# One channel of seven batches, loaded by itself and transformed in one run

## The chip, the cores and the metric

The kernel runs on one core of a Trainium2 chip. The core has five engines that work side by side and wait for each other by semaphores: TensorE (PE; its weight loads are listed apart as PEld), VectorE (DVE), ScalarE (ACT), GpSimd (POOL), and SyncE (SP), which here only issues DMAs. The DMAs run on 16 DMA engines. The metric is the time of one execution on the device in microseconds (us), the median of several runs.

## What is computed

The input x has 8 batches of 3008 rows and 256 columns ("channels"). Each batch goes through a Fourier transform over its rows and one over its channels, of which the real part is kept; the result goes, row by row, through a gated network:

```python
X = np.fft.fft(x, axis=1)
X = np.fft.fft(X, axis=2)
y = X.real.reshape(8 * 3008, 256)
gate = np.maximum(y @ w_gate, 0.0)      # 256 -> 1536
val  = y @ w_val
out  = gate * val @ w_out               # 1536 -> 256
```

## The kernel before

The transform over the channels is folded into the weights (tiles WA, WB, WM). The transform over the rows is done as matrix products with tables of cosines and sines (`tabC`, `tabS`). Before these products the rows of a batch are folded: rows 1, 2, 3, ... of the first half (tile XD, loaded in order) are added to the same rows counted from the end (tile XG, "mirrored", loaded from a reversed copy `xr` in DRAM), then halves are added and subtracted (tile AA, also called PQ), and channels d and 256 - d are added (tiles F) and subtracted (tiles G). So 128 or 129 channels are left of 256; 128 of them are the stationary operand of the products. Channel 128 is its own mirror image; it is the 129th and has no room in the 128.

For that channel batches 1 to 7 have products of their own. POOL computes `c128p` from column 128 of XG (line 187) and writes it, with signs, into the tile FN (line 188), in the slot of the batch. FN holds batches in pairs. For each pair, TensorE runs 12 products (line 656, `nyquist_steps`): 6 pieces of rows by 2 families of output rows, each with 4 stationary columns and 376 or 377 moving columns of `tabC`. Their results are copied to a small tile N (line 665, ScalarE; line 663, VectorE, once) and written to the DRAM tensor `ch` (lines 672 and 673, `keep_nyquist`), from where each batch reads its row (lines 1052 and 1055). The runs of 12 stand in batch 0 (for batch 1), and in batches 1, 3 and 5 (for the next two each). In batches 1, 3 and 5 they come after 18 of the 24 steps of the next batch's transform; the table `DFT_ODD` says after which tile of the network how many steps are done, `DFT_EVEN` the same for the other batches.

The order of instructions on each engine is written out by hand (a manual schedule): the generator lists steps of several kinds (`todo_dft`, `todo_out`, `todo_fold`), and after each tile of the network takes some from each list. Every engine then works through its own list in order. The folds of batches 1 and 2 are put on POOL at once during batch 0 (`run_fold(99)`), those of later batches step by step behind POOL's part in each tile (line 971), by an estimated cost written beside each step.

SP issues nearly all DMAs, in the order in which the generator came to them: loads of XD (lines 94 and 100), the reversed copies (`reverse`, line 133, two batches ahead), their one-row complement (`reverse_0`, line 137), loads of XG (line 142), output rows (line 754) and the rows of channel 128. Eight semaphores go round: each DMA waits until the one eight places before it has landed. Four buffers hold output rows on their way out (tile os, line 744).

During batch 0, `turns_and_rows` (line 490) issues the loads for batch 1 and the reversed copy for batch 2.

The functions that the change touches:

Of the kernel before, what the change touches and what calls it, by code (L numbers as in the profile page):

```python
# [34 lines left out]
def kernel(  # L35
# [46 lines left out]

    FF = [single(f"F{i}", [128, 2, 3, 2, 129], BF16) for i in range(2)]
    GG = [single(f"G{i}", [128, 2, 3, 2, 128], BF16) for i in range(2)]
    FN = single("FN", [128, 2, 3, 2, B // 2, 2, 2], BF16)

# [33 lines left out]
    def load_upward(t, r, queue):  # L122
        first = H - 128 - 128 * t - r * (H // 2)
        queue.dma_start(out=XG[:, r, t, :, :].rearrange("p a d -> p (a d)"), in_=pairs[first:first + 128, :])

    PC, NC = 64, 6
    xr = nc.dram_tensor("xr", (B, 2, NC, PC, 2 * D), F32).ap()
# [49 lines left out]
    def fold_steps(b):  # L177

        e, p, ts = nc.gpsimd, slice(0, 128), slice(0, 3)
        steps = [(1.1, lambda r=r, t=t: fold_a(e, p, r, t)) for t in range(3) for r in range(2)]  # L180
        if b == 1:
            steps.insert(0, (0.0, lambda: e.tensor_copy(go[:, 1:2], go[:, 0:1])))
        steps += [(0.2, lambda: e.tensor_tensor(XG[:, :, :, ::-1, 0], XG[:, :, :, ::-1, 0], XD[:, :, :, :, 0], op=ALU.add))]

        def channel_128():
            for i in range(2):
                e.tensor_tensor(c128p[:, i], XG[:, 0, :, ::-1, 128], XG[:, 1, :, ::-1, 128], op=SIGN[i])
            e.tensor_tensor(FN[:, :, :, :, b // 2, :, b % 2].rearrange("p i t q h -> p i (t q) h"),
                            c128p[:].rearrange("p i t q -> p i (t q)").unsqueeze(3).to_broadcast([128, 2, 6, 2]), sg[:], op=ALU.mult)
        steps.append((0.5, channel_128))  # L190
        if b + 1 < B:
            steps.append((0.0, lambda: reverse_0(b + 1) if b else None))
        for t in range(3):
            for i in range(2):
                steps.append((1.1, lambda i=i, t=t: fold_pq(e, p, i, t)))
                if (t, i) == (1, 0) and b + 1 < B:
                    steps.append((0.0, lambda: (load_rows(b + 1), load_last(b + 1))))

        def small():
            for i in range(2):  # L200
                e.tensor_tensor(PQ[:, i, :, :, 0], XG[:, 0, :, ::-1, 0], XG[:, 1, :, ::-1, 0], op=SIGN[i])
            zero = PQ[:, :, :, :, 0:1].rearrange("p i t q d -> p (i t q) d")
            e.tensor_tensor(FF[b % 2][:, :, :, :, 0:1].rearrange("p i t q d -> p (i t q) d"), zero, zero, op=ALU.add)
        steps.append((0.6, small))
        last = []
        for fam in (1, 0):
            last.append((1.7, lambda fam=fam: fold_f(e, p, ts, fam, b)))
            last.append((1.7, lambda fam=fam: fold_g(e, p, ts, fam, b)))
        if b + 1 < B:
            last.insert(3, (0.0, lambda: load_reversed(b + 1)))  # L210
        if b + 2 < B:
            last.append((0.0, lambda: reverse(b + 2)))
        return steps + last
# [22 lines left out]
    kvec = single("kvec", [128, NK])  # L236
    dvec = single("dvec", [128, 129], pool=st_)
    go = single("go", [128, 2])
    c128p = single("c128p", [128, 2, 3, 2])
    sg = single("sg", [128, 2, 6, 2])  # L240

    odd_k, even_k = slice(NE, NK), slice(0, NE)
    order, even_order = (1, 0, 3, 2, 5, 4), (1, 3, 5, 0, 2, 4)
# [84 lines left out]
    quotient(2)  # L328
    nc.vector.scalar_tensor_tensor(us[:, 5:6], in0=pidx[:], scalar=120.0, in1=us[:, 5:6], op0=ALU.is_lt, op1=ALU.mult)
    nc.vector.memset(FN[:], 0.0)  # L330
    quotient(5)
    quotient(4)
    nc.vector.memset(XD[96:128, :, 2, 1, :], 0.0)
# [98 lines left out]
    iota(kvec[:, 0:NE], [[2, NE]], 0, 0)  # L432
    nc.gpsimd.memset(sg[:], 2.0)
    for i in range(2):
        nc.gpsimd.memset(sg[:, i, 0::2, i:i + 1], -2.0)
    spare = AA[:].rearrange("p r t q d -> p (r t q d)")

    def even_turns(n, c):
# [51 lines left out]
    def turns_and_rows():  # L490
        load_rows(1)
        load_last(1)
        load_mirror_0(1)
        for n, c in enumerate(even_order):
            even_turns(n, c)
            if n == 1:
                minus_v(nc.gpsimd, 1)
            if n:
                load_mirror(1, (n - 1) // 2, (n - 1) % 2)
        load_mirror(1, 2, 1)  # L500
        reverse(2)

# [137 lines left out]
                    steps += part  # L642
        return steps

    def nyquist_steps(g, N):

        def one():
            if not paired:
                flush()
            d = psD.tile([128, 512], F32, name="d", tag="d")  # L650
            for k in range(6):
                t, par = k // 2, k % 2
                rows = slice(0, ROWS[par][t])
                for fam in range(2):
                    p, cols = slice(32 * fam, 32 * fam + 4), (slice(0, NE), slice(NE, NK))[fam]
                    nc.tensor.matmul(d[p, 0:NE - fam], lhsT=FN[rows, fam, t, par, g].rearrange("p s b -> p (s b)"),  # L656
                                     rhs=tabC[rows, 2 * t + par, cols], start=(k == 0), stop=(k == 5))

            def keep():
                for fam in range(2):  # L660
                    p = slice(32 * fam, 32 * fam + 4)
                    if fam and not paired:
                        nc.vector.tensor_scalar(N[p, 0:NJ], d[p, 0:NJ], scalar1=1.0, op0=ALU.mult, scalar2=None)
                    else:
                        nc.scalar.copy(N[p, 0:NE - fam], d[p, 0:NE - fam])
            evict.insert(0, keep)
        return [one]

    def keep_nyquist(g, N):
        W = 4 * NJ + 1  # L670
        for fam in range(2):
            nc.sync.dma_start(out=dram(ch128, 2 * g * W + 2 * (1 - fam) * NJ, [[NJ, 2], [W, 2], [1, NJ]]), in_=N[32 * fam:32 * fam + 4, 0:NJ])
        nc.sync.dma_start(out=ch128[2 * g:2 * g + 2, 4 * NJ:4 * NJ + 1], in_=N[2:4, NJ:NE])

    def new_uv():
        return [up.tile([128, 4 * NJ + 2], BF16, name=n, tag=n) for n in ("U", "V")]
# [104 lines left out]
    def gate_128():  # L781
# [2 lines left out]
            nc.tensor.matmul(p[:, f:f + 1], lhsT=WB[0][0:1, f * 128:(f + 1) * 128], rhs=one[:], start=True, stop=True)  # L784
        nc.vector.tensor_scalar(b2[:], p[:, 0:NF], scalar1=1.0, op0=ALU.mult, scalar2=None)
    more[(2, 2)] = [gate_128]

    DFT_0 = (0, 0, 0, 0, 0, 3, 0, 0, 4, 3, 3, 0), (0, 0, 0, 0, 0) + (1,) * 7, (3, 3, 3, 3, 3, 3, 0, 0, 0, 0, 0, 0)

    DFT_EVEN = (3, 0, 3, 0, 0, 0) * 4 + (0,) * 12  # L790
    DFT_ODD = (3, 0, 3, 0, 0, 0) * 3 + (1, 0, 3, 0, 3, 0, 0) + (0,) * 11
    todo_out, todo_dft, todo_fold = [], [], []
    credit, paired = 0, False
    pending = None
# [221 lines left out]
    for b in range(B):  # L1016
# [4 lines left out]
        for blk, block in enumerate(blocks):  # L1021
# [13 lines left out]
            if blk == (0 if b else 2) and b + 1 < B:  # L1035
                Un, Vn = new_uv()
                todo_dft = dft_steps(b + 1, Un, Vn, (1, 0), now=not b)
                CBn = up.tile([128, 4 * NJ + 2], BF16, name="CB", tag="CB")
                uv[b + 1] = Un, Vn, CBn
                steps, todo_dft = todo_dft, []  # L1040
                if b == 0 or b % 2:
                    g, N = (b + 1) // 2, rp.tile([36, NE], BF16, name="N", tag="N", bufs=1)
                    todo_dft = nyquist_steps(g, N)

                    def keep(N=N, g=g):
                        flush()
                        keep_nyquist(g, N)
                    first = 0 if b == 0 else 18
                    steps[first] = lambda step=steps[first], keep=keep: (keep(), step())

                def row_128(b=b, CBn=CBn):
                    nc.sync.dma_start(out=CBn[:, 0:4 * NJ + 1], in_=dram(ch128, (b + 1) * (4 * NJ + 1), [[0, 128], [1, 4 * NJ + 1]]))

                def row_0(b=b, Vn=Vn):
                    nc.sync.dma_start(out=Vn[0:1, 0:4 * NJ + 1], in_=ch128[b + 1:b + 2, :])
                for at, f in ((6 if b == 0 else 21, row_128), (21, row_0)):
                    steps[at] = lambda step=steps[at], f=f: (f(), step())
                todo_dft = todo_dft + steps if b == 0 else steps[:18] + todo_dft + steps[18:]
            per_tile = -(-len(todo_out) // NF)
            paired = b > 0  # L1060
            if (b, blk) == (0, 0):
# [26 lines left out]
            else:  # L1088
                for fi in range(NF):
                    at = NF * blk + fi  # L1090
                    cur = ahead.pop(0)
                    add_h(cur, hs)
                    ahead.append(next(tiles, None))
                    outs = per_tile
                    if (b, blk) == (B - 1, 2) and fi > 8:
                        outs = (10, 11, 17)[fi - 9]
                        if fi == 9:
                            rest = out_steps(b, block, hs)
                            early, rest = rest[:10] + rest[12:16], rest[10:12] + rest[16:]
                            todo_out += early  # L1100
                    pending = slot(cur, *ahead, outs, .72)
                    run(todo_dft, DFT_ODD[at] if b % 2 else DFT_EVEN[at])
            if b or blk > 1:
                run(todo_out, len(todo_out))
            if blk == len(blocks) - 1 or (b, blk) == (0, 1):
# [41 lines left out]
```

## Time and profile before

| | |
|---|---|
| median of 3 runs | 633.44 us (633.27 to 633.48) |
| the profiled execution | 633.34 us |
| its span, first to last instruction | 631.6 us |
| busy, of the span | TensorE 620.3, VectorE 554.2, POOL 506.9, ScalarE 446.3 us |
| granted TensorE clock | full |
| products of channel 128 | 48, at 69.66, 144.40, 292.44 and 440.27 us (12 each) |
| DMA packets | 64,196, of them 19,802 under 512 bytes |

A line of groups or of the timeline begins with the place in the code (L656 is line 656) and the engine, names the operation, and shows output <- input with the shape. In the timeline the first number is the start in us from the beginning of the span and the second the busy time; "x12" means that twelve instructions in a row are merged. In a table of stretches each engine's busy us stand in the order PE, PEld, DVE, ACT, POOL, then the granted clock, the share of the 16 DMA engines in use, and GB/s. The busy time of TensorE is modelled from the starts of products, which overlap; so what a product costs is read from one start to the next.

### The profile page before, as it was taken

The numbers are of one execution on the slowest core, as the hardware profiler recorded it, in microseconds if no ns is written. First come the engines' busy times: TensorE is split into PE (matmuls) and PEld (weight loads), VectorE is DVE, ScalarE is ACT, GpSimd is POOL, SyncE is SP. The second block draws the span as 40 slices with busy tenths as digits, with TensorE's granted clock in tenths as the row PEclk, the third lists the DMA queues.
The fourth block names the chain that finished last, engine by engine and source line by source line (L and its number), as shares of the span: only waits on it lengthen the run. The fifth ranks groups of instructions, "written<-read, shape, count | busy, mean of one in ns | idle before, by whom it ended". The sixth has DMA issues, their size and how long they took to land.

```text
span 631.6 us, 12458 instructions
## 1 busy us (share of the span) xinstructions
PE 620.3 (98%) x4090; PEld 398.8 (63%) x4137; DVE 554.2 (88%) x984; ACT 446.3 (71%) x810; POOL 506.9 (80%) x495
## 2 busy tenths in 40 slices
PE   8999999999999999999999999999999999999997
PEld 2566666566666666666666666666666666666666
DVE  8896676998999899988999999898899989999991
ACT  6786667777777767777677767776777777777762
POOL 8988992998989998798889989699896566666660
PEclk9999999999999999999999999999999999999999
DMA  9954653714272427314272425321221111211113
GB/s 239 209 194 133 170 184 101 194 50 144 84 196 93 133 70 177 117 51 143 70 198 86 135 76 111 75 63 38 75 59 38 43 59 56 53 41 51 50 46 99
DMA packets 64196, 66.32 MB, mean 105 GB/s; under 512 B 19802, under 2 KB 47226, under 8 KB 64131
## 3 DMA queue, kind: packets, MB, share of 16 engines
q1 hardware_dynamic: 59715, 59.96, 32.9%
q0 software_dynamic: 3984, 4.92, 4.0%
q8 instruction: 32, 0.52, 0.4%
q10 hardware_dynamic: 432, 0.66, 0.3%
q14 instruction: 33, 0.27, 0.1%
HBM read 41.77 MB, written 34.13 MB: 120 GB/s over the span
## 4 chain that ended last, share of the span: by engine, by line
PE 90%; DVE 5%; issue 2%; POOL 1%; DMA 1%; ACT 1%; DVEq 0%; POOLq 0%; ACTq 0%
PE o L731 36%; PE v L820 10%; PE v L825 10%; PE g L959 8%; PE p L966 8%; PE v L819 8%; PE d L538 4%; DVE h L855 3%; PE p L825 1%; PE p L819 1%; PE p L820 1%; DMA XG<-in_x_dram,gidx 1%; DVE r L970 1%; DVE h L844 1%; PE d L656 1%
## 5 line engine op out<-in xcount | busy, mean ns | idle before, releaser
L971 POOL TENSOR_TENSOR r<-r 128x512 f32<-128x512 f32 (+1 forms) x252 | 314.2, 1252 | 100.2 <-DVE r L970 99.9
L855 DVE SCALAR_TENSOR_TENSOR h<-r,v 128x512 bf16<-128x512 f32 (+1 forms) x504 | 318.6, 674 | 40.9 <-PE v L825 29.4
L731 PE MATMUL o<-wo,h 128*128 128x256 bf16 x2172 | 330.9, 273 | 0.0
L731 PEld LDWEIGHTS <-h 128*128 128x128 bf16 x2220 | 216.6, 98 | 112.4 <-issue 1.5
L954 ACT ACTIVATE p<-CB,b 128x512 f32<-128x512 bf16 (+1 forms) x252 | 172.5, 684 | 73.6 <-DVE r L970 72.2
L962 ACT COPY r<-g 128x512 f32<-128x512 f32 (+1 forms) x252 | 145.4, 577 | 67.1 <-PE g L959 58.7
L970 DVE SCALAR_TENSOR_TENSOR r<-r,p 128x512 f32<-128x512 f32 (+1 forms) x252 | 168.9, 670 | 0.6 <-ACT r L962 0.6
L820 PE MATMUL v<-V,WB 128*128 128x512 bf16 (+3 forms) x296 | 108.7, 367 | 2.3
L825 PE MATMUL v<-V,WM 128*128 128x512 bf16 (+1 forms) x252 | 94.5, 375 | 1.1 <-DVE h L855 0.7
L959 PE MATMUL g<-V,WM 128*128 128x512 bf16 (+1 forms) x252 | 94.6, 375 | 0.4 <-ACT r L962 0.3
L966 PE MATMUL p<-U,WA 128*128 128x512 bf16 (+1 forms) x252 | 94.6, 375 | 0.0
L819 PE MATMUL v<-U,WA 128*128 128x512 bf16 (+3 forms) x252 | 92.0, 365 | 0.0
L844 DVE TENSOR_TENSOR h<-r,v 128x376 bf16<-128x376 f32 (+1 forms) x88 | 44.9, 543 | 16.4 <-PE v L825 9.2
L819 PEld LDWEIGHTS <-WA 128*128 128x128 bf16 x347 | 33.8, 97 | 40.2 <-issue 11.6
L820 PEld LDWEIGHTS <-WB 128*128 128x128 bf16 x347 | 33.8, 97 | 34.2 <-DVE WB L381 0.6
L744 ACT COPY os<-o 128x512 f32<-128x512 f32 x92 | 52.6, 572 | 3.6 <-issue 3.0
L151 POOL TENSOR_TENSOR XG<-XG,XD 128x510 f32<-128x510 f32 x42 | 52.9, 1268 | 0.0
L835 ACT ACTIVATE r<-p 128x376 f32<-128x376 f32 (+1 forms) x80 | 38.1, 485 | 18.7 <-PE p L825 9.9
L159 POOL TENSOR_TENSOR AA<-XG 128x510 f32<-128x510 f32 x42 | 45.3, 1089 | 0.0
L959 PEld LDWEIGHTS <-WM 128*128 128x128 bf16 x252 | 24.6, 98 | 6.4 <-issue 1.0
L966 PEld LDWEIGHTS <-WA 128*128 128x128 bf16 x252 | 24.6, 98 | 3.4 <-issue 0.5
L825 PEld LDWEIGHTS <-WM 128*128 128x128 bf16 x252 | 24.6, 98 | 2.9
(178 smaller groups left out, 417.4 us busy)
## 6 DMA issues: line engine op xcount, KB each, us to landing
out_dram<-os SPq DMA_DIRECT2D x124, 128.0 KB
xr<-in_x_dram SPq DMA_DIRECT2D x12, 768.0 KB
XG<-xr SPq DMA_DIRECT2D x12, 768.0 KB
XD<-in_x_dram SPq DMA_DIRECT2D x15, 512.0 KB
out_dram<-os SPq DMA_DIRECT2D x35, 112.0 KB
XD<-in_x_dram SPq DMA_DIRECT2D x8, 448.0 KB
CB<-ch SPq DMA_DIRECT2D x7, 376.2 KB
out_dram<-os SPq DMA_DIRECT2D x13, 96.0 KB
```

The costliest lines, as they stand in the source:

```text
L151: e.tensor_tensor(XG[p, r, t, ::-1, 1:D], XG[p, r, t, ::-1, 1:D], XD[p, r, t, :, D - 1:0:-1], op=ALU.add)
L731: nc.tensor.matmul(st["p"][0:m, q, :], lhsT=lhs(f), rhs=wo[:, f, :], start=(f == 0 and not (early and q)), stop=(f == NF - 1), skip_group_ ...
L819: nc.tensor.matmul(bank[:, 0:st["n"]], lhsT=WA[i][:, st["f"]], rhs=st["us"], start=True, stop=False)
L820: nc.tensor.matmul(bank[:, 0:st["n"]], lhsT=WB[i][:, st["f"]], rhs=st["vs"], start=False, stop=True)
L825: nc.tensor.matmul(bank[:, 0:st["n"]], lhsT=W[i][:, st["f"]], rhs=v, start=False, stop=True, skip_group_check=True)
L855: nc.vector.scalar_tensor_tensor(half_h(st, sign), in0=st["s"][1 + sign][:, 0:n], scalar=0.0, in1=st["v"][:, 0:n], op0=ALU.max, op1=ALU.mult)
L954: nc.scalar.activation(st["p"][:, 0:st["n"]], st["c"], ACTF.Copy, scale=b2[:, st["fi"]:st["fi"] + 1])
L959: nc.tensor.matmul(st["g"][:, 0:n], lhsT=WM[0][:, st["f"]], rhs=st["vs"], start=True, stop=True)
L962: nc.scalar.copy(q[:, 0:n], st["g"][:, 0:n])
L966: nc.tensor.matmul(st["p"][:, 0:n], lhsT=WA[0][:, st["f"]], rhs=st["us"], start=False, stop=True, skip_group_check=True)
L970: nc.vector.scalar_tensor_tensor(sp[:, 0:n], in0=q[:, 0:n], scalar=-0.5, in1=st["p"][:, 0:n], op0=ALU.mult, op1=ALU.add)
L971: nc.gpsimd.tensor_tensor(sm[:, 0:n], sp[:, 0:n], q[:, 0:n], op=ALU.add)
```

## The change

Channel 128 of batches 1 to 7 no longer comes from XG. A new function loads it from x by itself: for each row piece, its 4-byte elements of 7 batches and 2 halves (14 columns) into a new tile CX. The mirrored rows go through a small DRAM tensor `cr`: the channel is first written there in reversed order (14 columns by 752 rows), and later read into the second half of CX. The first part (six DMAs) is issued on SP at the end of `turns_and_rows`, the second (three DMAs, after the first has landed) with tile 6 of the second segment of batch 0. POOL folds all seven batches at once (five instructions), as a step of batch 1's fold, between its small step and the folds to F and G. FN holds all eight batches side by side (16 columns; those of batch 0 stay zero). One run of 12 products in batch 0 transforms them all, one pair of evictions copies them, and three DMAs write them to `ch`. The runs in batches 1, 3 and 5 are gone, and all batches follow `DFT_EVEN`.

```diff
-    FN = single("FN", [128, 2, 3, 2, B // 2, 2, 2], BF16)
+    FN = single("FN", [128, 2, 3, 2, 2, B], BF16)
+    CX = single("CX", [128, 2, 3, 2, 2 * (B - 1)])
...
+    cr = nc.dram_tensor("cr", (H // 2, 2 * (B - 1)), F32).ap()
+
+    def load_channel_128(mirrored):
+
+        n, queue = 2 * (B - 1), nc.sync
+        rows, first, last = dict(allow_slow_non_contiguous=True), (S + 1) * D + 128, (S + H - 1) * D + 128
+        if not mirrored:
+            queue.dma_start(out=dram(cr, 0, [[1, n], [n, H // 2]]), in_=dram(x, last, [[H * D, n], [-D, H // 2]]), **rows)
+            for t in range(2):
+                queue.dma_start(out=CX[:, 0, t], in_=dram(x, first + 256 * t * D, [[2 * D, 128], [D, 2], [H * D, n]]), **rows)
+            for a in range(2):
+                queue.dma_start(out=CX[0:120 - a, 0, 2, a], in_=dram(x, first + (512 + a) * D, [[2 * D, 120 - a], [H * D, n]]), **rows)
+            queue.dma_start(out=CX[120:121, 1, 2, 1], in_=dram(x, (S + H) * D + 128, [[S * D, B - 1], [-H * D, 2]]), **rows)
+        else:
+            for t in range(3):
+                m = (128, 128, 120)[t]
+                queue.dma_start(out=CX[0:m, 1, t], in_=dram(cr, 256 * t * n, [[2 * n, m], [n, 2], [1, n]]))
...
         def channel_128():
+            n = B - 1
+            halves = [CX[:, k].rearrange("p t q (b r) -> p (t q b) r", r=2) for k in range(2)]
+            e.tensor_tensor(halves[0], halves[0], halves[1][:, :, ::-1], op=ALU.add)
+            parts = CX[:, 1].rearrange("p t q n -> p (t q n)").rearrange("p (m b) -> p m b", b=n)
             for i in range(2):
-                e.tensor_tensor(c128p[:, i], XG[:, 0, :, ::-1, 128], XG[:, 1, :, ::-1, 128], op=SIGN[i])
-            e.tensor_tensor(FN[:, :, :, :, b // 2, :, b % 2].rearrange("p i t q h -> p i (t q) h"),
-                            c128p[:].rearrange("p i t q -> p i (t q)").unsqueeze(3).to_broadcast([128, 2, 6, 2]), sg[:], op=ALU.mult)
-        steps.append((0.5, channel_128))
+                e.tensor_tensor(parts[:, 6 * i:6 * i + 6].rearrange("p m b -> p (m b)"), halves[0][:, :, 0], halves[0][:, :, 1], op=SIGN[i])
+            for s in range(2):
+                e.tensor_tensor(FN[:, :, :, :, s, 1:B].rearrange("p i t q b -> p (i t q) b"),
+                                parts,
+                                sg[:, s].unsqueeze(2).to_broadcast([128, 12, n]), op=ALU.mult)
...
         steps.append((0.6, small))
+        if b == 1:
+            steps.append((1.5, channel_128))
...
+    nc.vector.memset(CX[:, :, 2], 0.0)
...
         reverse(2)
+        load_channel_128(False)
...
-                    p, cols = slice(32 * fam, 32 * fam + 4), (slice(0, NE), slice(NE, NK))[fam]
-                    nc.tensor.matmul(d[p, 0:NE - fam], lhsT=FN[rows, fam, t, par, g].rearrange("p s b -> p (s b)"),
+                    p, cols = slice(32 * fam, 32 * fam + 2 * B), (slice(0, NE), slice(NE, NK))[fam]
+                    nc.tensor.matmul(d[p, 0:NE - fam], lhsT=FN[rows, fam, t, par].rearrange("p s b -> p (s b)"),
                                      rhs=tabC[rows, 2 * t + par, cols], start=(k == 0), stop=(k == 5))
...
-            nc.sync.dma_start(out=dram(ch128, 2 * g * W + 2 * (1 - fam) * NJ, [[NJ, 2], [W, 2], [1, NJ]]), in_=N[32 * fam:32 * fam + 4, 0:NJ])
-        nc.sync.dma_start(out=ch128[2 * g:2 * g + 2, 4 * NJ:4 * NJ + 1], in_=N[2:4, NJ:NE])
+            nc.sync.dma_start(out=dram(ch128, 2 * (1 - fam) * NJ, [[NJ, 2], [W, B], [1, NJ]]), in_=N[32 * fam:32 * fam + 2 * B, 0:NJ])
+        nc.sync.dma_start(out=ch128[0:B, 4 * NJ:4 * NJ + 1], in_=N[B:2 * B, NJ:NE])
...
+    more.setdefault((1, 6), []).append(lambda: load_channel_128(True))
...
-    DFT_ODD = (3, 0, 3, 0, 0, 0) * 3 + (1, 0, 3, 0, 3, 0, 0) + (0,) * 11
...
-                if b == 0 or b % 2:
-                    g, N = (b + 1) // 2, rp.tile([36, NE], BF16, name="N", tag="N", bufs=1)
-                    todo_dft = nyquist_steps(g, N)
+                if b == 0:
+                    N = rp.tile([32 + 2 * B, NE], BF16, name="N", tag="N", bufs=1)
+                    todo_dft = nyquist_steps(N)
...
-                todo_dft = todo_dft + steps if b == 0 else steps[:18] + todo_dft + steps[18:]
+                todo_dft = todo_dft + steps
...
-                    run(todo_dft, DFT_ODD[at] if b % 2 else DFT_EVEN[at])
+                    run(todo_dft, DFT_EVEN[at])
```

More of the change, by code (lines that the diff above doesn't have):

```diff
@@ L238 @@
     go = single("go", [128, 2])
-    c128p = single("c128p", [128, 2, 3, 2])
-    sg = single("sg", [128, 2, 6, 2])
+    sg = single("sg", [128, 2, 12])
     odd_k, even_k = slice(NE, NK), slice(0, NE)
@@ L434 @@
     for i in range(2):
-        nc.gpsimd.memset(sg[:, i, 0::2, i:i + 1], -2.0)
+        nc.gpsimd.memset(sg[:, i, 6 * i:6 * i + 6:2], -2.0)
     spare = AA[:].rearrange("p r t q d -> p (r t q d)")
@@ L643, in dft_steps, with nyquist_steps @@
         return steps
-    def nyquist_steps(g, N):
+    def nyquist_steps(N):
         def one():
@@ L660, in keep @@
                 for fam in range(2):
-                    p = slice(32 * fam, 32 * fam + 4)
+                    p = slice(32 * fam, 32 * fam + 2 * B)
                     if fam and not paired:
@@ L667, in nyquist_steps, with keep_nyquist @@
         return [one]
-    def keep_nyquist(g, N):
+    def keep_nyquist(N):
         W = 4 * NJ + 1
         for fam in range(2):
-            nc.sync.dma_start(out=dram(ch128, 2 * g * W + 2 * (1 - fam) * NJ, [[NJ, 2], [W, 2], [1, NJ]]), in_=N[32 * fam:32 * fam + 4, 0:NJ])
-        nc.sync.dma_start(out=ch128[2 * g:2 * g + 2, 4 * NJ:4 * NJ + 1], in_=N[2:4, NJ:NE])
+            nc.sync.dma_start(out=dram(ch128, 2 * (1 - fam) * NJ, [[NJ, 2], [W, B], [1, NJ]]), in_=N[32 * fam:32 * fam + 2 * B, 0:NJ])
+        nc.sync.dma_start(out=ch128[0:B, 4 * NJ:4 * NJ + 1], in_=N[B:2 * B, NJ:NE])
     def new_uv():
@@ L1040, with keep @@
                 steps, todo_dft = todo_dft, []
-                if b == 0 or b % 2:
-                    g, N = (b + 1) // 2, rp.tile([36, NE], BF16, name="N", tag="N", bufs=1)
-                    todo_dft = nyquist_steps(g, N)
-                    def keep(N=N, g=g):
+                if b == 0:
+                    N = rp.tile([32 + 2 * B, NE], BF16, name="N", tag="N", bufs=1)
+                    todo_dft = nyquist_steps(N)
+                    def keep(N=N):
                         flush()
-                        keep_nyquist(g, N)
-                    first = 0 if b == 0 else 18
-                    steps[first] = lambda step=steps[first], keep=keep: (keep(), step())
+                        keep_nyquist(N)
+                    steps[0] = lambda step=steps[0], keep=keep: (keep(), step())
                 def row_128(b=b, CBn=CBn):
```

## The prediction

> **What bounds the kernel now.** I read the page first (busy shares, the chain that ended last), then the two lines of the products that the change thins out, then the order of instructions around them on TensorE, and last the stretch of batch 0 in which the new loads must arrive, on POOL, SP and the DMA engines.
>
> ```profile
> PE 620.3 (98%) x4090; PEld 398.8 (63%) x4137; DVE 554.2 (88%) x984; ACT 446.3 (71%) x810; POOL 506.9 (80%) x495
> PE 90%; DVE 5%; issue 2%; POOL 1%; DMA 1%; ACT 1%; DVEq 0%; POOLq 0%; ACTq 0%
> ```
>
> TensorE is busy for 98% of the span and is 90% of the chain, so TensorE time taken out of the steady part should shorten the kernel, if no other engine is next in line there. The channel-128 products, and one of their four places in order of time:
>
> ```profile
> L656 PE MATMUL d<-tabC,FN x48: 320/323/325, 69.7 to 441.1; 128*4 128x377 bf16 x16, 128*4 128x376 bf16 x16, 120*4 120x377 bf16 x4, 120*4 120x376 bf16 x4
> ...
> 292.02 0.49 PE L731 MATMUL o<-wo,h 128*128 128x256 bf16 x3
> 292.44 1.13 PE L656 MATMUL d<-tabC,FN 128*4 128x377 bf16 x12
> 293.50 0.39 PE L959 MATMUL g<-V,WM 128*128 128x512 bf16 x1
> 284.00:300.00 16.00, 15.90 (x110) 9.91 (x110) 13.59 (x25) 11.94 (x22) 14.21 (x13) 1.00 0.44 142
> ```
>
> 48 products have a duration of 323 ns each, but the two families overlap: twelve of them hold TensorE from 292.44 to 293.50, 1.06 us. The stretch around them (the last line: PE, PEld, DVE, ACT and POOL busy out of 16 us) has TensorE at 15.90 and VectorE at 13.59: VectorE is not next in line there.
>
> **What is removed.** Three of the four runs of twelve (36 products) go, at 144.40, 292.44 and 440.27 us. Before each of them three products of L731, 0.108 us each, should have ended 0.32 us after their start (292.02 + 0.32 = 292.34); the run starts 0.10 us later. So a run costs 1.06 + 0.10 = 1.16 us, and three cost 3.48 us, all of it on the chain. The fourth run stays; 16 stationary columns in place of 4 change no moving column, and I price it at the same 1.06 us. Also removed: six evictions of N on ScalarE (0.46 us each), nine DMAs to ch and seven times 0.61 us on POOL (two of 0.20, one of 0.25). I price these at nothing: in that stretch ScalarE has 4 us of 16 free, and POOL's next release of TensorE is covered by TensorE's own queue. The different place of the dft products in odd batches (three by three in both patterns) is priced at nothing too; TensorE has no idle time there to gain or lose.
>
> **What is added, small.** A memset of CX (56 words; the 96 words of FN took 0.14 us) in VectorE's opening: at most 0.1 us, and VectorE has a gap of 0.24 us ahead of 13.96 us that can hold it. I take 0.05.
>
> **What is added, large: the loads.** SP issues six gathers right behind the reversed copy of batch 2, that is at 32.5 us:
>
> ```profile
> 30.97 1.54 SPq L133 DMA_DIRECT2D xr<-in_x_dram  x2
> 41.81 11.21 SPq L754 DMA_DIRECT2D out_dram<-os  x8
> ...
> 33.00:36.00 3.00, 3.00 (x24) 2.15 (x22) 2.91 (x6) 2.34 (x7) 2.71 (x4) 1.00 0.37 132
> ...
> 57.91 0.22 POOL L183 TENSOR_TENSOR XG<-XG,XD 128x12 f32<-128x12 f32 x1
> 58.10 0.36 POOL L187 TENSOR_TENSOR c128p<-XG 128x6 f32<-128x6 f32 x2
> ...
> 65.46 0.24 POOL L203 TENSOR_TENSOR F<-AA 128x12 bf16<-128x12 f32 x1
> 65.62 1.67 POOL L166 TENSOR_TENSOR F<-AA 128x768 bf16<-128x768 f32 x1
> 67.25 1.67 POOL L175 TENSOR_TENSOR G<-AA 128x762 bf16<-128x762 f32 x1
> ...
> 69.66 1.13 PE L656 MATMUL d<-tabC,FN 128*4 128x377 bf16 x12
> ...
> 72.15 0.32 PE L538 MATMUL d<-tabS,G 128*128 128x376 bf16 x1
> ```
>
> Elements of one channel lie 1 KB apart, so each is a 4-byte piece of its own: 14 x 752 = 10,528 into cr, and 3,584 + 3,584 + 1,680 + 1,666 + 14 = 10,528 into CX, 21,056 in all. In the trace a DMA leaves one packet per contiguous piece (128 of 132 bytes for the 128x33 columns of LB). The reversed copy ahead of them has 6 blocks and keeps 0.37 of 16 engines busy, that is six; its 2,048-byte packets take 84 ns and run until about 45 us in the packet records. If the outer count sets the engines in the same way, cr runs on 14, the 120-row piece on 15 and the 119-row piece on 7, and the fullest engine has 752 + 224 + 224 + 112 + 238 + 7 = 1,557 packets, behind the reversed copy. Spread evenly it would be 1,316.
>
> The price of a 4-byte packet from DRAM is the unknown of this forecast; the kernel before has none. Rows, by packet duration: 16 bytes between SBUF tiles 7 ns; 128 bytes from DRAM to DRAM (the reversed rows 0) 11 ns; 132 bytes of LB 14 ns; an output row of 1 KB 46 ns. A load of 2,048 bytes at 84 ns shows that DRAM itself keeps up with 24 bytes per ns and engine. I take 11 ns, the only small row that both reads and writes DRAM, and keep 7 and 46 ns as ends. The gathers then end at 45 + 1,557 x 0.011 = 62.1 us (ends: 55.9 and 116.6). Behind them SP issues the three mirrored loads of CX from cr: three issues of 0.4 us and about 1.2 us from an issue to its first packet (LB at 381.24 and 382.42), so 2.5 us, and CX is there at 64.6.
>
> POOL comes to the new channel_128 when its small step ends, now 65.70 - 0.61 = 65.1 us. It arrives after the loads, by half a microsecond. The five new POOL instructions, priced from 128x6 at 0.20, 128x24 at 0.25 and 128x510 at 1.05 to 1.26 us, take about 1.6 us in place of 0.61. FN is then there at 66.7 (needed at 69.66) and the first G at 65.1 + 1.6 + 1.67 + 1.67 = 70.0 (needed at 72.15): cover of 3.0 and 2.1 us, so no stall. If that cover were gone, every microsecond would be one on TensorE, whose order is fixed, and behind the waiting POOL stand the folds of batch 1, six casts of WM and the fold of batch 2.
>
> SP's queue: from its ninth DMA on each waits for the one eight before it, so the second group of output rows, the third, reverse_0, XD and XG of batch 2 and the next reversed copy wait for the gathers. XD moves from 58 to about 66 us, and XG's end from about 72 to 78; the fold of batch 2 starts at 76.17 now. It may slip 2 us, and POOL then idles 10.6 us before 105.15, which hides it. The fifth output copy (69.92) needs the first copy's buffer, whose rows now leave behind the gathers at about 63: hidden by 7 us.
>
> **Sum.** 3.48 - 0.05 = 3.4 us off the profiled execution of 633.34 us (span 631.6 and 1.7 around it): 629.9. The median of the runs is 633.44, 0.1 above it, so 630.0 us.
>
> **Against the change, from the notes.** The Trainium skill, DMA: Bandwidth & Descriptors, section "Rules for kernel authors", says that a strided last dimension becomes one descriptor per element and should be rearranged to be contiguous. By its count the sum above is the same; it gives no price. Its section "Why small descriptors are slow (HBM only)" puts the penalty on HBM and exempts traffic between SBUFs: my 7 and 14 ns rows are of the exempt kind, and no run here shows 4-byte reads from DRAM. That supports the first rival below.
>
> **Rivals.**
> - The loads come late (slower). Place: POOL's first new instruction. The stall begins when CX lands after 67.25 us (72.15 - 4.9), and it eats the whole gain when CX lands after 70.7, that is gathers ending at 68.2: (68.2 - 45) / 1,557 = 14.9 ns a packet. Reads of DRAM that are each waited for, or partial writes of cr that meet in the same line, would do that. Halfway between 11 and 46 ns, at 28 ns, the gathers end at 88.6, CX lands at 91.1, the stall is 23.9 us and the time 633.4 - 3.4 + 23.9 = 654; at 46 ns it is 682. For it: break-even is only 4 ns above my price, and no row shows 4 bytes from DRAM. Against it: the rows from 16 to 132 bytes are all at 7 to 14 ns.
> - VectorE takes over as the bound where the products were, and the time stays at 633.4. Against it: 25 us of VectorE's idle time from 140 to 600 us is a wait for TensorE's L825, none of TensorE's own but 0.5 us is a wait for VectorE. The same time comes out if the loads are late by just the gain.
> - The change does only a part of what it says: the seven batches' products could be no cheaper in one run. With 16 columns in place of 4 in the weight load and the same moving columns I see no way; if the run took twice as long, the time would be 631.2.
>
> **Chances.** The forecast 0.46, with a range of its own from 629.0 (another 1 us from the freed POOL and ScalarE) to 632.0; late loads beyond the gain 0.44; no change, by VectorE or by a delay of about the gain, 0.09; a smaller gain 0.01, counted with the forecast's side. A change within 0.2% (1.3 us) can't be told from none here. The range reaches up into the late loads to 660 us, a packet of about 32 ns; above that I leave 0.15. Faster 0.47, same 0.09, slower 0.44.
>
> **What would show it.** Right: twelve products of channel 128 in all, TensorE's neighbours L731 and L959 closed up at three places, the new POOL run starting near 65 us with no idle time before it. Wrong: POOL idle before the new channel_128 with a DMA as releaser, TensorE idle at the remaining run or at the first dft product behind it, and SP's output rows late between 42 and 70 us.

## The result, and the profile after

The changed kernel takes 659.61 us (median of 4 runs, 658.91 to 662.04), the kernel before 633.46 us. The ratio is 1.042, with a 95% interval from 1.0393 to 1.0448: slower by 4.2%, where a gain of 0.5% was forecast. The profiled execution took 659.12 us, 25.8 us more than the profiled one of before.

The busy shares of the page and the chain of work that ended last, of the kernel after:

```profile
PE 620.7 (94%) x4056; PEld 399.5 (61%) x4101; DVE 554.3 (84%) x985; ACT 444.0 (68%) x804; POOL 504.6 (77%) x479
PE 80%; SPq 9%; DVE 4%; POOL 3%; DMA 2%; issue 2%; ACT 1%; DVEq 0%; ACTq 0%; POOLq 0%
PE o L758 32%; PE v L847 9%; PE v L852 9%; PE g L986 8%; PE p L993 8%; PE v L846 7%; SPq L136 7%; PE d L565 4%; DVE h L882 3%; DMA CB<-ch 1%; POOL XG L478 1%; POOL AA L178 1%; DVE r L997 1%; PE v L373 1%; DMA XG<-in_x_dram 1%
```

TensorE's busy time is nearly what it was, but its share of the span fell from 98 to 94%. A new member has entered the chain: SP's queue, at line 136, the gathers into CX. The next lines are taken from the list of waits of the kernel after, of TensorE, POOL and ScalarE (the line that waited, what it waited for, us in total, times, longest):

```profile
PE d L683 <- POOL FN L212: 20.5, 1, 20.5
PE g L852 <- ACT r L862: 5.2, 1, 5.2
POOL XG L170 <- DMA XG<-in_x_dram,gidx: 8.9, 5, 6.7
POOL CX L207 <- DMA CX<-cr: 14.4, 1, 14.4
ACT os L771 <- DMA out_dram<-os: 15.5, 1, 15.5
ACT p L981 <- DMA CB<-ch: 6.0, 1, 6.0
```

TensorE stands still twice. First for 20.5 us at the one run of channel-128 products, for FN, for which POOL waits for CX. Then for 5.2 us in the last tile of batch 0, behind ScalarE, which waits for CB, the channel-128 rows of batch 1. The order of events, from the timelines of SP, POOL and TensorE:

```profile
32.82 2.97 SPq L134 DMA_DIRECT2D cr<-in_x_dram  x1
35.84 42.80 SPq L136 DMA_DIRECT2D CX<-in_x_dram  x2
78.69 2.69 SPq L138 DMA_DIRECT2D CX<-in_x_dram  x2
81.42 1.86 SPq L139 DMA_DIRECT2D CX<-in_x_dram  x1
83.39 2.49 SPq L781 DMA_DIRECT2D out_dram<-os  x6
...
74.14 0.24 POOL L227 TENSOR_TENSOR F<-AA 128x12 bf16<-128x12 f32 x1
88.77 0.36 POOL L207 TENSOR_TENSOR CX<-CX 128x84 f32<-128x84 f32 x1 [14.39 <-DMA CX<-cr]
...
90.43 2.06 PE L683 MATMUL d<-tabC,FN 128*16 128x377 bf16 x12 [20.50 <-POOL FN L212]
```

SP hands over the gather into cr at 32.82 and is then held for 42.8 us at the next two gathers; the first output rows leave at 83.39 in place of 41.81. POOL itself reaches its new step at 74.4 and not at 65.1, because the mirrored rows of batch 1, which GpSimd's own queue loads, came late too. The reversed copy of batch 2, on SP's queue in front of the gathers, was held as well: in the trace's semaphore records, in which each DMA engine of a transfer reports its share as landed, its second half is there at 60.5 us and not at 46.3. The fourteen engines of cr are through one after another, between 59.6 and 77.9 us. The stretches 60 to 70 us of before and after (PE, PEld, DVE, ACT, POOL busy, clock, share of the DMA engines in use, GB/s), before first:

```profile
60.00:70.00 10.00, 9.93 (x81) 6.27 (x80) 6.76 (x15) 6.58 (x16) 9.92 (x11) 1.00 0.70 209
```

```profile
60.00:70.00 10.00, 9.86 (x76) 6.24 (x74) 6.78 (x15) 6.58 (x15) 7.81 (x8) 1.00 0.85 6
```

In the kernel after the DMA engines are 85% in use and move 6 GB/s.

The sum closes: the two stalls are 25.7 us. Behind each of them the granted clock is down for some microseconds (0.50 from 90.40 to 92.40, 0.53 from there to 95.00, and 0.52 from 129.60 to 132.50): the twelve products take 1.99 us from start to next start in place of 1.06, what follows up to the first dft product 2.56 in place of 1.43, and the stretch behind the second stall 2.95 in place of about 1.6; together 3.4 us. Less the 3.5 us at which the prediction counts the three runs that are gone, that is 25.6 of the 25.8 us. The Trainium skill, TensorE: Matmul & The Clock Gate, section "What's actually happening", says that an idle window of some 3.4 us throttles the array to half clock; here twelve products at a granted clock of 0.50 after 20.5 us of idling agree with it.

### The profile page after: what moved, and what is told of

It is laid out like the page before. It is cut to its first block, busy times and chain, and to the rows that moved or that the text cites. A ratio compares the mean times of both kernels' runs of the same rounds, so it can differ in the third digit from the quotient of the medians.

```text
span 657.4 us, 12370 instructions
## 1 busy us (share of the span) xinstructions
PE 620.7 (94%) x4056; PEld 399.5 (61%) x4101; DVE 554.3 (84%) x985; ACT 444.0 (68%) x804; POOL 504.6 (77%) x479
## 4 chain that ended last, share of the span: by engine, by line
PE 80%; SPq 9%; DVE 4%; POOL 3%; DMA 2%; issue 2%; ACT 1%; DVEq 0%; ACTq 0%; POOLq 0%
PE o L758 32%; PE v L847 9%; PE v L852 9%; PE g L986 8%; PE p L993 8%; PE v L846 7%; SPq L136 7%; PE d L565 4%; DVE h L882 3%; DMA CB<-ch 1%; POOL XG L478 1%; POOL AA L178 1%; DVE r L997 1%; PE v L373 1%; DMA XG<-in_x_dram 1%
## 5 line engine op out<-in xcount | busy, mean ns | idle before, releaser
L882 DVE SCALAR_TENSOR_TENSOR h<-r,v 128x512 bf16<-128x512 f32 (+1 forms) x504 | 318.5, 673 | 37.3 <-PE v L852 25.8
L862 ACT ACTIVATE r<-p 128x376 f32<-128x376 f32 (+1 forms) x80 | 38.1, 486 | 19.7 <-PE p L852 9.5
```

Of the source, the lines that this page charges most:

```text
L882: nc.vector.scalar_tensor_tensor(half_h(st, sign), in0=st["s"][1 + sign][:, 0:n], scalar=0.0, in1=st["v"][:, 0:n], op0=ALU.max, op1=ALU.mult)
```

## Experiments

Two theories stand against each other at the start. One is that the pieces written to DRAM, the gather into cr, are slow; which of such writes are slow is then a question of its own. The other is that any gather of 4-byte pieces at this place is slow, by its reads, by their number or by its place in the queue.

A time below without a ratio is that of a single execution. The four executions of the changed kernel lie 3.1 us apart, so a difference of that size between single executions shows nothing.

### The gain by itself, and the gathers into SBUF alone

`no_loads` leaves out every load of channel 128:

```diff
...
-        load_channel_128(False)
...
-    more.setdefault((1, 6), []).append(lambda: load_channel_128(True))
...
-    nc.vector.memset(CX[:, :, 2], 0.0)
+    nc.vector.memset(CX[:], 0.0)
```

> Leaves out all loads of channel 128 (CX is zero, so channel 128 of batches 1 to 7 counts as zero), and keeps the one run of twelve products and all of POOL's new work. Theory: the saving of three runs of twelve is whole, 3.4 us: 630.0 us, and the 26 us of loss are all the loads'. Rival (VectorE or POOL takes over as the bound): 632.5 to 634 us.

Measured: 631.04 us, ratio 0.9959 (0.9945 to 0.9973). The whole loss is the loads'. The saving is 2.4 us, by the interval 1.7 to 3.5.

`no_cr` keeps the gathers from x into CX and leaves out cr and what is read from it, so that the mirrored half of CX stays zero:

```diff
-            queue.dma_start(out=dram(cr, 0, [[1, n], [n, H // 2]]), in_=dram(x, last, [[H * D, n], [-D, H // 2]]), **rows)
...
-        else:
-            for t in range(3):
-                m = (128, 128, 120)[t]
-                queue.dma_start(out=CX[0:m, 1, t], in_=dram(cr, 256 * t * n, [[2 * n, m], [n, 2], [1, n]]))
...
```

> Leaves out the reversed copy cr and the mirrored half of CX (it stays zero); the five gathers of 10,528 four-byte pieces from x into CX stay at their place behind the reversed copy. Theory (the pieces written to DRAM are slow, those read from DRAM into SBUF are not): a packet of 4 bytes at about 9 ns, CX there at about 53 us, no wait on POOL, 630.0 us. Rival (any gather of 4-byte pieces at this place is slow, by its reads or by the queue): half the pieces, half the time, CX there at about 60 us and POOL's fold of batch 1 late by some microseconds: 633 to 640 us.

Measured: 630.17 us, ratio 0.9950 (0.9933 to 0.9967). SP and POOL in this run:

```profile
32.80 14.00 SPq L134 DMA_DIRECT2D CX<-in_x_dram  x2
46.84 5.57 SPq L136 DMA_DIRECT2D CX<-in_x_dram  x2
52.46 1.75 SPq L137 DMA_DIRECT2D CX<-in_x_dram  x1
54.31 0.86 SPq L775 DMA_DIRECT2D out_dram<-os  x2
...
65.02 0.24 POOL L221 TENSOR_TENSOR F<-AA 128x12 bf16<-128x12 f32 x1
65.21 0.36 POOL L201 TENSOR_TENSOR CX<-CX 128x84 f32<-128x84 f32 x1
```

POOL's new step starts behind the small step with no wait, at the 65.1 us of the prediction. The 10,528 pieces read from DRAM into SBUF cost the kernel nothing. Nor does it cost anything that SP is held until 54.31, where its first output row now leaves, 12.5 us later than before. The intervals of the two savings, 2.4 and 3.3 us, overlap; the forecast 3.4 lies inside both, at the edge of the first.

### Which writes to DRAM are slow

`cr_own_run` lays cr out as 14 runs of 752 elements, so that each column has a stretch of memory of its own, and `cr_own_line` gives each element 64 bytes of its own. Both read cr back in 4-byte pieces.

```diff
-    cr = nc.dram_tensor("cr", (H // 2, 2 * (B - 1)), F32).ap()
+    cr = nc.dram_tensor("cr", (2 * (B - 1), H // 2), F32).ap()
...
-            queue.dma_start(out=dram(cr, 0, [[1, n], [n, H // 2]]), in_=dram(x, last, [[H * D, n], [-D, H // 2]]), **rows)
+            queue.dma_start(out=dram(cr, 0, [[H // 2, n], [1, H // 2]]), in_=dram(x, last, [[H * D, n], [-D, H // 2]]), **rows)
...
```

```diff
-    cr = nc.dram_tensor("cr", (H // 2, 2 * (B - 1)), F32).ap()
+    cr = nc.dram_tensor("cr", (H // 2, 2 * (B - 1) * 16), F32).ap()
...
-            queue.dma_start(out=dram(cr, 0, [[1, n], [n, H // 2]]), in_=dram(x, last, [[H * D, n], [-D, H // 2]]), **rows)
+            queue.dma_start(out=dram(cr, 0, [[16, n], [16 * n, H // 2]]), in_=dram(x, last, [[H * D, n], [-D, H // 2]]), **rows)
...
```

> cr is laid out as 14 runs of 752 elements, so each of the 14 columns is written in ascending 4-byte steps to its own 3 KB, and no two columns share a line; the second part then reads 10,528 four-byte pieces from cr instead of 376 pieces of 112 bytes, some 6 us more. Theory A (14 columns written into the same 56 bytes at the same moment hold each other up): cr done in some 10 us, CX there by 62 to 68 us, 630 to 636 us. Theory B (every 4-byte write to DRAM costs, wherever it lands): cr takes as long as now, 35 us and more, and 660 to 668 us.

> Each element of cr stands alone in 64 bytes, so that no two writes meet in a line at all; the second part reads 10,528 four-byte pieces from cr, some 6 us more. Theory A (writes that meet in a line hold each other up): cr done in some 10 us, 630 to 636 us. Theory B (every 4-byte write to DRAM costs): 660 to 668 us. If the columns' own runs are fast and this is slow, or the other way round, it is the number of lines touched or the order within one column that counts.

Measured: 721.52 and 648.85 us. SP's queue, first with the own runs, then with the own lines:

```profile
36.61 97.87 SPq L136 DMA_DIRECT2D CX<-in_x_dram  x2
...
139.82 0.39 SPq L781 DMA_DIRECT2D out_dram<-os  x1
```

```profile
36.15 26.57 SPq L136 DMA_DIRECT2D CX<-in_x_dram  x2
...
68.25 0.86 SPq L781 DMA_DIRECT2D out_dram<-os  x2
```

Neither theory as written holds. Keeping the 14 columns apart made it worse, not better, so it is not only that different columns meet; the worst layout is the one in which one column writes 16 neighbours one after the other. Where no two writes share 64 bytes it is cheapest. One reading fits all three: writes that land close to others that have just been written hold each other up, most when they follow one another in one engine's stream, less when they come from 14. It is argued, not shown. The cheap layout also spreads the same pieces over 16 times the memory (674 KB in place of 42), which no run tells apart from its 64 bytes to each piece.

### The same pieces into SBUF

`cr_in_sbuf` sends the same reads, on the same 14 columns, to an unused tile, leaves out cr and what is read from it, and keeps the mirrored half of CX at zero:

```diff
-            queue.dma_start(out=dram(cr, 0, [[1, n], [n, H // 2]]), in_=dram(x, last, [[H * D, n], [-D, H // 2]]), **rows)
+            queue.dma_start(out=LB[0:n].rearrange("p f c -> p (f c)")[:, 0:H].bitcast(F32), in_=dram(x, last, [[H * D, n], [-D, H // 2]]), **rows)
...
```

> The same 14 by 752 reversed reads from x on the same 14 engines, but written to an unused tile in SBUF (14 partitions, runs of 752) and not to DRAM; the mirrored half of CX stays zero, so its part of channel 128 is left out. Theory (the writes to DRAM are the cost): the gather takes 752 x 9 ns, about 7 us after the reversed copy, 630.2 us. Rival (reading 4-byte pieces in this order on 14 engines is the cost): 650 to 660 us.

Measured: 643.36 us; SP is through at 68.17. Both expectations were off: it is better than cr by 16 us, but not free. `cr_near` reads the columns 64 bytes apart:

```diff
-            queue.dma_start(out=LB[0:n].rearrange("p f c -> p (f c)")[:, 0:H].bitcast(F32), in_=dram(x, last, [[H * D, n], [-D, H // 2]]), **rows)
+            queue.dma_start(out=LB[0:n].rearrange("p f c -> p (f c)")[:, 0:H].bitcast(F32), in_=dram(x, last, [[H * D, n], [-16, H // 2]]), **rows)
```

> cr_in_sbuf with the reads of each column 64 bytes apart in place of 1 KB (other elements of x, so the unused tile holds something else; the mirrored half of CX stays zero, as there). In cr_in_sbuf SP is through with the gathers 13.9 us later than without any copy, about 18 ns for each of 752 pieces of an engine, twice the 9 ns of the gathers into CX. Theory (the reads, 1 KB apart, are what makes these pieces dearer): about 9 ns again, SP through at about 61 us in place of 68, and 631 to 638 us. Rival (it is the 4-byte writes one after the other into one partition, or the 14 engines): SP through at about 68 us, 641 to 645 us.

Measured: 644.04 us, SP through at 69.13. Reads 64 bytes apart are no cheaper than reads 1 KB apart.

All these runs can be put on one scale: when SP is through with the gathers (the start of its first output row), less the 54.31 us of `no_cr`, divided by the pieces that the fullest engine has in addition (752, if 14 columns use 14 engines; 672 in `turned`, below). The last column is an estimate, since other traffic runs beside the pieces.

| layout of the extra 10,528 pieces | SP through, us | more than without | ns a piece |
|---|---|---|---|
| into SBUF, 128 partitions (`turned`) | 59.66 | 5.4 | 8 |
| into SBUF, 14 partitions | 68.17 | 13.9 | 18 |
| into DRAM, 64 bytes each | 68.25 | 13.9 | 19 |
| into DRAM, rows of 14 (the change) | 83.39 | 29.1 | 39 |
| into DRAM, runs of 752 | 139.82 | 85.5 | 114 |

The landings of the changed kernel agree with the fourth row: the 4-byte packets start at 38.1 us and the fourteen engines have written their 752 pieces between 59.6 and 77.9, which is 29 to 53 ns a piece. The table splits the delay of the change in two. Of its 29.1 us, 13.9 are there with the same pieces sent to 14 partitions of SBUF, and with 64 bytes to each piece writing to DRAM costs no more than that; the other 15.2 come with the layout of cr.

### What is held: the queue or the engines

`before_cr` is the kernel before with cr and the gather into it added, behind the reversed copy of batch 2. Nothing reads cr.

```diff
         reverse(2)
+        n = 2 * (B - 1)
+        nc.sync.dma_start(out=dram(cr, 0, [[1, n], [n, H // 2]]), in_=dram(x, (S + H - 1) * D + 128, [[H * D, n], [-D, H // 2]]), allow_slow_non_contiguous=True)
```

> The kernel before, with the gather into cr alone added behind the reversed copy; nothing reads cr. Theory: the slow writes hold the DMA engines, so the mirrored rows of batch 1 (GpSimd's queue) land 7 to 9 us late, POOL's folds of batch 1 slip by as much, and TensorE stalls about 6 us at the first dft product: 638 to 642 us. Rival (only the wait of POOL for CX costs): 633.5 us.

Measured: 653.04 us, 19.6 us lost with no one waiting for the data. Its SP queue, its stretch from 60 to 70 us and its waits:

```profile
32.50 2.96 SPq L504 DMA_DIRECT2D cr<-in_x_dram  x1
41.75 36.38 SPq L757 DMA_DIRECT2D out_dram<-os  x8
60.00:70.00 10.00, 9.93 (x80) 6.26 (x79) 6.70 (x15) 6.56 (x14) 8.20 (x11) 1.00 0.80 10
PE p L828 <- ACT r L838: 8.2, 1, 8.2
PE g L828 <- ACT r L838: 7.3, 1, 7.3
ACT os L747 <- DMA out_dram<-os: 8.8, 1, 8.8
ACT p L957 <- DMA CB<-ch: 8.1, 1, 8.1
```

The late mirrored rows that I expected are there (POOL's third fold of batch 1 waits 6.4 us for them), but the two stalls come from two things that I had not expected: ScalarE finds no free output buffer (8.8 us), and CB is late (8.1 us).

`before_cr_act` and `after_act` issue the gather into cr from ScalarE's queue at 33 us, in the kernel before and in the changed one (where it then no longer stands on SP):

```diff
+    def copy_channel_128():
+        n = 2 * (B - 1)
+        nc.scalar.dma_start(out=dram(cr, 0, [[1, n], [n, H // 2]]), in_=dram(x, (S + H - 1) * D + 128, [[H * D, n], [-D, H // 2]]), allow_slow_non_contiguous=True)
+    more.setdefault((0, 9), []).append(copy_channel_128)
```

> The kernel before, with the gather into cr added on ScalarE's queue at 33 us; nothing reads cr. Theory (cr blocks the queue that it stands in): SP's loads go on, and of the 19.6 us that the same gather cost on SP only the 3 us of its issue on ScalarE and the late mirrored rows of batch 1 stay: 636 to 642 us. Rival (the DMA engines themselves are held): 650 us and more.

> The changed kernel with the gather into cr issued from ScalarE's queue at 33 us in place of SP's; the five gathers into CX stay on SP. Theory (cr holds what is queued behind it on SP): SP's rows and loads are no longer blocked, but POOL still waits for cr, which is done at 65 to 75 us: 640 to 652 us. Rival (cr holds the DMA engines, whoever issues it): 656 to 662 us.

Measured: 659.29 and 662.12 us. The theory that the loss comes from the blocked queue falls. In `before_cr_act`, where SP issues nothing slow, its output rows are late all the same:

```profile
42.03 42.75 SPq L755 DMA_DIRECT2D out_dram<-os  x8
84.83 1.22 SPq L138 DMA_DIRECT2D xr<-in_x_dram  x2
```

The 42.75 us are not one issue. The second and third of the eight issues last 7.2 and 6.9 us. Then SP waits until 71.36 for the reversed copy of batch 2, whose large pieces SP had issued at 31 us: its second half is there at 71.35, against 46.3 in the kernel before. The last issue, at 84.45, waits for ScalarE's copy. In `before_cr`, where the pieces stand on SP's own queue, the issue of the first output row alone lasts 29.5 us. So the queue decides what is held first, and the time is lost either way: pieces on one queue slow down the transfers of the others. That points to the DMA engines, or to the memory behind them, which the runs do not tell apart. The Trainium skill, DMA: Bandwidth & Descriptors, section "Issuing engines are not separate DMA queues", says that DMAs started by ScalarE, SP or GpSimd run on the same 16 DMA engines and interleave there; these two runs agree, since neither is faster than its counterpart with SP (653.04 and 659.61 us).

### The second stall

`after_cb` lists the load of CB one step earlier, ahead of the XD loads of batch 3, which wait for POOL's fold of batch 2:

```diff
-                for at, f in ((6 if b == 0 else 21, row_128), (21, row_0)):
+                for at, f in ((5 if b == 0 else 21, row_128), (21, row_0)):
```

> The changed kernel with that same one step. Theory: its second stall (5.2 us and some 1.3 us at half clock) goes, the first stays: 652 to 654 us. Rival (the second stall comes from full DMA engines): 658 to 660 us.

Measured: 657.08 us. TensorE's waits:

```profile
PE d L683 <- POOL FN L212: 23.0, 1, 23.0
PE g L986 <- DMA V<-ch: 0.9, 1, 0.9
```

The second stall is gone (5.2 us to 0.9), so its cause was the place of CB in SP's order. The time fell by 2 us alone, less than expected and within the spread of the changed kernel, because cr was slower in this execution (SP through at 85.92) and the first stall 2.5 us longer. What shows the cause is the wait that is gone, not the time.

### A version without cr

`turned` reads the mirrored rows in ascending order into a tile with the partitions reversed, and TensorE turns them:

```diff
-            queue.dma_start(out=dram(cr, 0, [[1, n], [n, H // 2]]), in_=dram(x, last, [[H * D, n], [-D, H // 2]]), **rows)
+            for t in range(3):
+                m = (128, 128, 120)[t]
+                for q in range(2):
+                    queue.dma_start(out=CM[128 - m:128, t, q], in_=dram(x, last - (256 * t + 2 * (m - 1) + q) * D, [[2 * D, m], [H * D, n]]), **rows)
...
+    def turn_128():
+        p = psD.tile([128, 512], F32, name="d", tag="d")
+        w = 12 * (B - 1)
+        nc.tensor.matmul(p[:, 0:w], lhsT=turned[:], rhs=CM[:].rearrange("p t q n -> p (t q n)"), start=True, stop=True)
+        nc.scalar.copy(CX[:, 1].rearrange("p t q n -> p (t q n)"), p[:, 0:w])
+    more[(2, 1)] = [turn_128, lambda: late_fold()]
```

Here `late_fold` lists batch 1's steps from channel_128 on, and the casts of WM, behind the turn.

> No DRAM tensor cr: the mirrored rows of channel 128 are read from x in ascending order into a tile CM with the partitions reversed (six gathers in place of one), TensorE turns the partitions round with one product against a reversed identity (84 columns, float32), ScalarE copies it to CX; POOL's folds behind it are listed after that. Theory (only 4-byte pieces written to DRAM are slow): 21,056 pieces into SBUF at 9 ns, the fullest engine done at 45 + 1,477 x 0.009 = 58.3 us, no wait, the saving of no_cr less the product and some 0.3 us: 630.2 to 631. Rival (the number of 4-byte pieces is what costs): twice the pieces of no_cr, gathers done beyond 65 us: 634 to 645 us.

Measured: 636.94 us, ratio 1.0054 (1.0039 to 1.0069); the profiled execution took 634.95. The gathers are done in time, POOL's new step starts at 64.96 with no wait. But SP is held until 59.66, XD and XG of batch 2 come late, POOL's fold of batch 2 starts at 80.75 in place of 76.17, and CB stands behind it:

```profile
PE g L858 <- ACT r L868: 3.6, 1, 3.6
ACT p L987 <- DMA CB<-ch: 4.4, 1, 4.4
```

`turned_cb` is `turned` with the one line of `after_cb`, the earlier load of CB.

> turned, and the load of CB for batch 1 listed one step earlier, so that it stands on SP ahead of the XD loads of batch 3, which wait for POOL. Theory (what is left of turned's loss is this one load, late behind POOL's late fold of batch 2: 3.6 us and a slow clock behind it): the stall goes, 630 to 631.5 us. Rival (the load is late because the DMA engines are full): 635 to 637 us as before.

Measured: 630.96 us, ratio 0.9961 (0.9947 to 0.9974), faster than both kernels. TensorE's largest wait from 25 to 200 us is 1.1 us:

```profile
PE g L992 <- DMA V<-ch: 1.1, 1, 1.1
```

## Why the prediction was wrong, step by step

- What bounds the kernel, and the products removed: right. The forecast saving of 3.4 us was measured at 3.3 (`no_cr`) and 2.4 us (`no_loads`); the two intervals overlap. VectorE did not take over, as the second rival would have it.
- The number of pieces: nearly right. The landings show 14 engines for cr, 16, 16, 15 and 7 for the gathers into CX and 7 for the last 14 pieces, so that an engine with a part in all has 1,552 packets and not 1,557. Their place was not right: the first 4-byte packets start at 38.1 us, beside the reversed copy, and not behind its end at 45.
- **The step that failed** is the price: "I take 11 ns, the only small row that both reads and writes DRAM", put on all 21,056 pieces alike. For pieces read from DRAM into CX it was nearly right: in the packet records of `cr_own_line`, while cr is read back into CX in 4-byte pieces, 3,600 of them start in the 2 us from 72 to 74, that is 8.9 ns on each of 16 engines. For the pieces of cr it was wrong by a factor of 3.5: about 39 ns. The 11-ns row was 16 pieces of 128 bytes, one on each engine; it could show neither what happens behind the sixteenth nor what 4-byte writes next to each other cost.
- The way of pricing failed with it: the rows were typical durations of packets. In the changed kernel 3,792 packets of 4 bytes start on SP's queue from 60 to 72 us: 85% of them last at most 10 ns, their mean is 40 ns and the longest lasts 1.46 us. The price is in the few that are held.
- The rival of late loads is what happened, at the place that it named, POOL's first new instruction. It gave writes that meet in the same line as a way to its 14.9 ns, which the three layouts fit. That its middle case, 654 us, came near the 659.6 is in part luck: 28 ns on 1,557 pieces is 43.6 us, while 39 ns on 752 and 9 on the other 805 is about 36, and the second stall and the slow clock, which made up for it, were in no case of the prediction. The measured time lies within the stated range only at its upper end of 660 us, which belonged to this rival and not to the forecast of a gain.
- "Gathers end at 62.1, CX is there at 64.6": it was there at 88.7.
- "POOL comes to channel_128 at 65.1": at 74.4, since the mirrored rows of batch 1 on GpSimd's queue came late, as they do in `before_cr` too, where the gather into cr is all that was added. The prediction counted the queue in front of the gathers, not what they do to the transfers of other queues.
- SP's queue, priced at nothing: "hidden by 7 us" for the output buffer, and for XD, XG and the fold of batch 2 an idle time of POOL "which hides it". With gathers that end at 62 the fold of batch 2 starts late all the same (`turned`: 4.6 us, forecast 2), and CB, which I did not name among what stands behind it, costs a stall of 3.6 us there and of 5.2 us in the changed kernel. With the gather into cr as slow as it was, such delays alone, with nobody waiting for cr, cost 19.6 us (`before_cr`), as much as three quarters of the loss.
- Of what would show it wrong, all three signs came: POOL idle before channel_128 with a DMA as releaser, TensorE idle at the remaining run, output rows late.
- The Trainium skill, DMA: Bandwidth & Descriptors, section "Why small descriptors are slow (HBM only)", exempts traffic between SBUFs from the penalty of small pieces. It pointed the right way: the rows from SBUF were not a price for DRAM. But reading from DRAM into 128 partitions, at 8 to 9 ns, was as cheap as those rows; writing to DRAM, at 19 to 114 ns, was not.

What stays open is why 752 pieces written to 14 partitions of SBUF cost 18 to 20 ns each and those written to 128 partitions 8 to 9. The distance of the reads made no difference (`cr_near`: 1 KB or 64 bytes); the number of engines, and consecutive writes into one partition, were not told apart. That writes close to each other are the cause of the 39 and 114 ns is argued from the three layouts; how close they must be was not measured, the memory that the layouts span was not told apart from it, and what in the memory system does it was not seen.

## What to carry to other kernels

A price for a small DMA piece holds for its kind alone: take it from a row with the same kind of target and with many pieces in a stream, as the time of the whole stream and not as a typical packet. Where there is none, 4-byte writes to neighbouring addresses in DRAM may cost several times the reads: here 39 and 114 ns against 8 to 9. A slow gather is not paid only by who waits for its data: count the loads of all queues that share the DMA engines with it, and follow each late load one step further to what stands behind it in its queue's order. If the data must be mirrored, reading it into SBUF in order and turning it on an engine was worth it here, once a load that had become late was moved (`turned_cb`): a product that is busy for 0.35 us and gathers that held SP 5.4 us longer took the place of writes that held it 29 us longer.

## What the runs showed of the hardware that I had not expected

- 4-byte writes to DRAM, as estimated in the table: about 19 ns a piece and engine with 64 bytes to each, 39 ns in rows of 14 shared by 14 columns, 114 ns in runs written in ascending order. 4-byte reads from DRAM into 128 partitions of SBUF: 8 to 9 ns. The typical 4-byte packet lasts 9 ns in the slow streams too.
- The issue of a DMA on SP can itself last for tens of microseconds when small pieces stand in front of it on its queue: 36.8 us for the first gather into CX, and 29.5 us for an output row of 128 KB in `before_cr`. With the pieces on ScalarE's queue the longest issue of an output row on SP was 7.2 us, but the large pieces of the reversed copy landed 25 us late.
- The DMA engines show as 80 to 85% in use while they move 6 to 10 GB/s (60 to 70 us in the changed kernel and `before_cr`): their share in use does not say how much they carry.
